# Operands of the Strassen-like groups loaded and split ahead, in a fused attention and MLP block on one core

## The chip, the cores and the metric

The kernel runs on one core of a Trainium2 chip. The metric is the device time of one execution in microseconds (us). The core's engines each work through an instruction queue of their own: TensorE (PE, matmuls), VectorE (DVE), ScalarE (ACT), GpSimd (POOL) and SyncE (SP). SP and POOL issue the DMAs of this kernel, SP nearly all the loads, POOL the adds into memory. All five queues are in order: an instruction that waits holds up what stands behind it.

## The reference

```python
def _A_ref(x, wqkv, wo):            # sliding, dilated local attention
    H, W, dil = 32, 8, 2            # S = 2048 tokens, D = 576, head size 18
    q, k, v = split(x @ wqkv)
    idx = pos[:, None] - arange(W) * dil           # 8 keys, each 2 back
    attn = softmax(q . k[idx] * Dh**-0.5, masked where idx < 0)
    return (attn . v[idx]) @ wo
def _B_ref(x, w1, w2, w3, w4):      # F = 4608
    h  = gelu(layernorm(x) @ w1)
    hs = shift_columns_by_tokens(h) @ w2
    x1 = x + hs
    return x1 + gelu(layernorm(x1) @ w3) @ w4
xn = layernorm(x)
return x + _A_ref(xn, wqkv, wo) + _B_ref(xn, w1, w2, w3, w4)
```

Most of the arithmetic is `gelu(. @ w3) @ w4`. Float32 operands are split into a rounded high part and a low part (their difference), and three products high x high, high x low, low x high stand for one product. Splits are ACT casts followed by DVE subtractions.

## The kernel before, in words

The stages follow each other in one program, whose instructions stand on each engine in the order in which the Python code emits them: order is set by hand.

1. q, k, v products and the two mixer products w1, w2, up to about 313 us. The normalised x1, transposed, is stored as `xn[0..3]`, one DRAM tensor per 512 tokens.
2. 48 *units* u = 0..47. A unit is one pair of 128-wide columns of F (`c`, 12 of them) by one block of 512 tokens (`b`). In unit u PE does the *ups* of u (28 matmuls, line 795), then the four *downs* of unit u-1 (12 matmuls each, line 814). Beside them DVE computes the attention piece by piece (generator `attention`, driven by `bg`); its operands q, k, v come from DRAM over SP, and its output goes to DRAM as `od`. `get_n(b)` loads `xn[b]` for a block's first use, `split_n` splits it. Between u = 5 and 20, sums of blocks of xn are made in DRAM (`td[sb, "T1".."T4"]`).
3. 12 *groups* q = 0..11 cover the other pairs of F columns. One group is a Strassen-like 2 by 2 product: seven products P1..P7 of 7 matmuls each (line 1020), then eight downs D0..D7, which are emitted in the next group (four of unit 47 in q = 0). Groups 0 to 5 take the first half of the tokens (sb = 0), 6 to 11 the second (sb = 1), with the pairs in reversed order. A half has seven operands: `B11` (in P1), `B21` (P2), `T2` (P6), `T1` (P5), `T3` (P7), `T4` (P4), `B22` (P3). `get_op` loads one (two DMAs: 128x2x512, then 96x1x512, which writes the last 32 rows three times), `split_op` splits it. For each pair, `load_pair` loads w3 (raw tile `w3st`, four DMAs), `split_a` makes `w3a`, `combine` and `split_s` make `w3s`; `load_w4` and `split_w4` do the same for w4. All the loads stand in SP's queue, all the casts in ACT's. `ORDER`, `ORDERS` and `plan` say behind which item each of them is emitted.
4. In groups 7 to 10 the attention's output is turned: `load_o` loads a tile of `od` into `big1`, `o_turn` transposes it on DVE into `big0`, `put` stores four of them to `xd`. In group 11 and behind it `read_xo` loads them back, `split_x` and `split_wo` split them and wo.
5. The last eight downs, then the wo products (line 212) and the output.

`negative z` in the code counts from the end: z = u - 48 for the units (z = -3 is unit 45), z = q - 12 for the groups (z = -1 is group 11). A down's output goes to SBUF by a DVE add (line 822), or, for ten of the sixteen token tiles, by an ACT copy to a staging slot (line 818) and an adding POOL DMA into `yd` in DRAM (line 819).

In the kernel before, T2 and T1 of the first half lie in one ring block, T4 and B22 in another, loaded when group 0 begins; for the second half B11 and B21 are loaded in group 4 into `big0` and `big1` (so that B11 and B21 are loaded again in group 6), the others in group 5, where their splits, as those of groups 6, stand beside the downs:

```python
        if q == 0:
            split_s(0)
            x1r = ring_block(("w", 1))
            area["T4"], area["B22"] = x1r[:, 0:5, :], x1r[:, 5:10, :]
            get_op(0, "B22")
            get_op(0, "T4")
            load_pair(1)
```

Of the kernel before, what the change touches and what calls it, by code (L numbers as in the profile page):

```python
# [57 lines left out]
def fused_block(ctx, tc, x, wqkv, wo, w1, w2, w3, w4, out):  # L58
# [476 lines left out]
    def load_w3p(c):  # L535
        st = wspool.tile([128, 4, 3, 128], F32, name="w3st").rearrange("p o s c -> p (o s) c")
        for i in range(2):
            load_w3f(2 * c + i, st[:, 5 * i:5 * i + 5])
# [131 lines left out]
    def attention(ap):  # L670
# [8 lines left out]
        def load(name, sel, g, lead):  # L679
            t = ap.tile([128, TPP + (halo if lead else 0), GC], F32, name=name)  # L680
            r = sel * NG + g
            sp.dma_start(t[:, (halo if lead else 0):, :],
                         qkvd[r, halo:, :].rearrange("(p j) d -> p j d", p=128))
# [28 lines left out]
        qs[0], ks[0] = load("q", 0, 0, False), load("k", 1, 0, True)  # L712
        vs[0] = load("v", 2, 0, True)
# [140 lines left out]
    area = {}  # L854

    def get_op(sb, k):
        n0, n1 = xn[2 * sb], xn[2 * sb + 1]
        src = {"B11": n0[0:HF], "B21": n0[HF:], "B22": n1[HF:]}.get(k)
        if src is None:
            src = td[sb, k]  # L860
        dst = area[k].bitcast(F32)
        sp.dma_start(dst[:, 1:3, :], src[0:256].rearrange("(k p) c -> p k c", p=128))
# [59 lines left out]


# [10 lines left out]
    for u, (c, b) in enumerate(units):  # L934
# [7 lines left out]
        for i in range(C):  # L942
# [4 lines left out]
            if (u, i) == (0, 0):  # L947
                get_n(2, x1n[2])
                load_w3p(1)
            for t in LATE.get((u, i), ()):  # L950
                n_turn(t, ntpool)
            if (u, i) == (0, 1):
                get_n(3, x1n[3])
            if (u, i) in ((1, 0), (2, 1)):
                split_n(u + 1, x1n[u + 1], 0, RT)
            if z == -2:
                split_op(("B11", "B21")[i])
            if z == -1:
# [25 lines left out]
        if z == -3:  # L984
            x2 = xp_tile(2)
            area["B11"], area["B21"] = x2[:, 0:5, :], x2[:, 5:10, :]
            get_op(0, "B11")
            get_op(0, "B21")
            x3 = xp_tile(3)
            area["T3"] = x3[:, 0:5, :]  # L990
            get_op(0, "T3")
        if z == -2:
            x0 = ring_block(("w", 0))
            area["T2"], area["T1"] = x0[:, 0:5, :], x0[:, 5:10, :]
            get_op(0, "T2")
            get_op(0, "T1")
        if 5 <= u < 21 and u % 2:
# [17 lines left out]
    def product(w, xk):  # L1015
        nps[1] += 1
        ps = qpc.tile([128, 512], F32, name=f"cc{nps[1] % 4}")
        for i, (a, v) in enumerate(HALVES):
            k = 128 if a else 96
            pe.matmul(ps, WX[w][:k, v, SLOT[w], :], area[xk][:k, a, :], start=i == 0, stop=i == len(HALVES) - 1)  # L1020
# [5 lines left out]
    x1r = None  # L1026
    otile, xo = {}, {}
    while not state["done"]:
        bg(1e9)
    apc.__exit__(None, None, None)  # L1030


    opc = tc.tile_pool(name="op", bufs=1, reuse_waits="tile")
    opool = opc.__enter__()

    def place(k):
        return opool.tile([128, 5, 512], F32R, name=f"big{k}")

    evc_pool = tc.tile_pool(name="evp", bufs=1, reuse_waits="tile")
    evp = evc_pool.__enter__()  # L1040
# [22 lines left out]
    def o_turn(t):  # L1063
        if t + 3 < NT:
# [7 lines left out]
              NWP: "P1 P2 P6 P5 D0 P7 D1 P4 D2 P3 D3 D4 D5 D6 D7"}  # L1072
    OPS = ("B11", "B21", "T2", "T1", "T3", "T4", "B22")
    for q in range(NQ):
# [50 lines left out]
        run = lambda f, *a: lambda: f(*a)  # L1125
        n = q + 1
        if q == 0:
            plan = {"D0": [run(load_w4, p)], "P5": [run(split_op, "B22")],
                    "P7": [gelu22], "D1": [run(split_op, "T4")],
                    "D2": [run(split_a, n), run(combine, n)], "P3": [run(split_s, n, (0, 1))],  # L1130
                    "P4": [run(split_s, n, (2,)), gelu12, low22],
                    "D3": [run(split_w4, p), low12, run(load_pair, 2)]}
        elif z < -1:
            plan = {"D3": [gelu22], "D4": [low22], "D5": [gelu12], "D6": [low12]}
            late = lambda it, *fs: plan.setdefault(it, []).extend(fs)
            if n != NWP:
                late("P2", run(split_a, n, (0, 1)))
                late("P6", run(split_a, n, (2,)))
                late("D1" if q == 1 else "D0", run(combine, n))
                both = q in (1, NWP)  # L1140
                late("P3", run(split_s, n, (0, 1) if both else (0,)))
                if not both:
                    late("D2", run(split_s, n, (1,)))
                late("D4" if q == 1 else "D3", run(split_s, n, (2,)))
            if q != NWP:
                plan.setdefault("D0", []).insert(0, run(load_w4, p))
                late("D6", run(split_w4, p, 0))
                late("D7", run(split_w4, p, 1))
            if z < -2 and q + 2 != NWP:
                late("D2", run(load_pair, q + 2))  # L1150
        else:
            plan = {"D1": [run(split_w4, p)], "D3": [gelu22], "D4": [gelu12, low22],
                    "D5": [low12]}
            for it, h in (("D2", 0), ("D4", 1)):
                plan.setdefault(it, []).append(lambda h=h: split_x(xo[0], h))
            for it, k in (("P3", 0), ("D3", 1), ("D6", 2)):
                plan.setdefault(it, []).append(run(split_wo, k))
        late = lambda it, *fs: plan.setdefault(it, []).extend(fs)

        def load_ahead(k, op):  # L1160
            x = ahead[op] = place(k)
            mine, area[op] = area[op], x
            get_op(1, op)
            area[op] = mine

        def split_ahead(op):
            mine, area[op] = area[op], ahead[op]
            split_op(op)
            area[op] = mine

        if q == NWP - 2:
            late("P2", run(load_ahead, 0, "B11"))
            late("D1", run(load_ahead, 1, "B21"))
            late("D4", run(split_ahead, "B11"))
            late("D7", run(split_ahead, "B21"))
        if q == NWP - 1:
            for it, k in zip(("P6", "P5", "P7", "P4", "P3"), OPS[2:]):
                plan.setdefault(it, []).insert(0, run(get_op, 1, k))
            for it, k in zip(("D2", "D4", "D6"), OPS[2:5]):
                late(it, run(split_op, k))  # L1180
        if q == NWP:
            late("P2", lambda: area.update(own), run(get_op, 1, "B11"), run(split_op, "T4"))
            late("P6", run(get_op, 1, "B21"))
            late("D0", run(split_op, "B22"))
            late("D5", run(split_op, "B11"))
            late("D7", run(split_op, "B21"))
# [3 lines left out]
        if -4 <= z <= -2:  # L1190
            plan.setdefault("P1", []).insert(0, run(put, ("o", z + 4)))
        if z == -2:
            late("D7", run(put, ("o", 3)))
# [5 lines left out]
        if z == -1:  # L1199
            late("P2", lambda: read_xo(0, xp_tile(2)))  # L1200
            late("P5", lambda: read_xo(1, ring_block(("o", 1))))
            late("P7", lambda: read_xo(2, xp_tile(3)))
            late("P3", lambda: read_xo(3, ring_block(("o", 3))))
# [112 lines left out]
```

## Time and profile before

| what | us |
|---|---|
| median of 3 runs (lowest, highest) | 1348.0 (1347.28, 1349.06) |
| the profiled execution's own time | 1341.79 |
| its span | 1340.0 |
| PE busy in the span | 1290.5 (96%) |
| DVE, ACT, POOL busy | 954.2, 550.9, 211.4 |
| one group with nothing in its way (q = 2, 978.15 to 1002.17) | 24.02 |

PE is busy nearly all the time, so time is lost where PE stands idle, and where it runs at a lower granted clock afterwards (column PEclk, 1.00 is full). A row of the timeline reads: start, duration, engine, line, operation, tiles, count, and in brackets the idle time before it with what ended it. A row of the windows reads: window, length, busy time of each engine with its count of instructions, granted clock, busy share of the 16 DMA engines (a row's share can pass 1 a little, since a packet counts in the slice in which it starts), GB/s.

### The profile page before, as it was taken

The page shows a single profiled execution, that of the slowest core. Times are in us where ns is not written, and L with a number is a line of the kernel's source. Part 1 is how long each engine was busy: PE and PEld are TensorE (multiplying, and loading weights), DVE is VectorE, ACT ScalarE, POOL GpSimd, SP SyncE. Part 2 cuts the span into 40 slices and gives each one's busy share as a digit, 9 for nine tenths or more (in the row PEclk, how much of TensorE's full clock was granted, in tenths as well). Part 3 has the DMA queues.
Part 4 walks back from the last instruction along what each step waited for, and adds up shares of the span by engine and source line. Part 5 has one row for each costly group of instructions (what it writes and reads, how often), then busy time and mean ns, then how long its engine had stood idle before and what let it go on. Part 6 is the DMA issues. An engine that isn't in the chain of part 4 may idle for free.

```text
span 1340.0 us, 19496 instructions
## 1 busy us (share of the span) xinstructions
PE 1290.5 (96%) x7594; PEld 1182.2 (88%) x7594; DVE 954.2 (71%) x1359; ACT 550.9 (41%) x882; POOL 211.4 (16%) x310
## 2 busy tenths in 40 slices
PE   9999999999899999999999999999899969989698
PEld 8999998898799989989999999888799958978698
DVE  6445525877378999899999999776766747657432
ACT  4332136446334434334343434336454645533520
POOL 2011100021112212122122221111021111211100
PEclk9999999999899999999999999999999989999799
DMA  7637874158786796978786874667566765878952
GB/s 214 154 100 158 185 161 145 48 152 220 211 204 105 151 270 102 228 134 185 146 188 129 172 156 77 130 140 167 126 107 157 149 161 123 189 168 193 292 140 80
DMA packets 195119, 211.66 MB, mean 158 GB/s; under 512 B 75906, under 2 KB 132162, under 8 KB 194898
## 3 DMA queue, kind: packets, MB, share of 16 engines
q1 hardware_dynamic: 165234, 149.65, 38.2%
q0 software_dynamic: 29792, 60.76, 30.2%
q8 instruction: 59, 0.97, 0.3%
q14 instruction: 34, 0.28, 0.1%
HBM read 114.43 MB, written 107.28 MB: 165 GB/s over the span
## 4 chain that ended last, share of the span: by engine, by line
PE 57%; issue 8%; DVE 2%; DMA 2%; SPq 2%; POOL 1%; ACT 1%; POOLq 0%; DVEq 0%; ACTq 0%
PE ps L814 27%; PE p L795 21%; PE cc L1020 5%; PE ps L212 4%; DMA w3st<-in_B_w_dram 1%; POOL yd L819 1%; SPq L890 1%; SPq L888 1%; DMA yd<-Y 1%; DVE prod L703 0%; PE p L1283 0%; DVE xt L587 0%; DVE Y L822 0%; ACT ev L818 0%; DVE Y L1024 0%
## 5 line engine op out<-in xcount | busy, mean ns | idle before, releaser
L814 PE MATMUL ps<-w,c 128*128 128x288 f32 x3456 | 483.9, 298 | 26.7 <-ACT Y L818 12.1
L814 PEld LDWEIGHTS ps<-w,c 128*128 128x128 f32 x3456 | 475.4, 191 | 38.4 <-ACT Y L818 12.9
L819 POOL DMA_DIRECT2D yd<-Y x128 | 112.7, 885 | 486.7 <-ACT Y L818 468.1
L818 ACT COPY Y<-ps 128x576 f32<-128x576 f32 x128 | 81.6, 639 | 170.4 <-PE ps L814 83.4
L789 DVE TENSOR_TENSOR c<-Y,c 128x512 fp32r<-128x512 f32 x144 | 98.6, 686 | 72.3 <-ACT Y L779 61.1
L778 ACT ACTIVATE c<-p 128x512 fp32r<-128x512 f32 x96 | 57.4, 597 | 194.6 <-PE p L795 194.6
L212 PE MATMUL ps<-WQ,xt 128*128 128x432 f32 x672 | 134.8, 360 | 0.0
L212 PEld LDWEIGHTS ps<-WQ,xt 128*128 128x128 f32 x672 | 125.7, 188 | 5.5
L822 DVE TENSOR_TENSOR Y<-ps,Y 128x576 f32<-128x576 f32 x108 | 81.1, 752 | 13.5 <-PE ps L814 13.3
L723 DVE TENSOR_TENSOR prod<-q,k 128x1152 f32<-128x1152 f32 x64 | 86.6, 1353 | 0.9
L726 DVE TENSOR_REDUCE L<-prod 128x64 f32<-128x1152 f32 x64 | 86.4, 1350 | 0.9
L819 POOL DMA_DIRECT2D yd<-ev x52 | 45.3, 876 | 249.2 <-ACT ev L818 247.6
L795 PE MATMUL p<-xt,w3a 128*128 128x512 f32 x336 | 78.9, 392 | 1.4 <-ACT Y L779 1.4
L795 PE MATMUL p<-x1n,w3a 128*128 128x512 f32 x336 | 79.3, 393 | 0.0
L795 PE MATMUL p<-x1n,w3s 128*128 128x512 f32 x336 | 78.7, 391 | 0.0
L795 PE MATMUL p<-xt,w3s 128*128 128x512 f32 x336 | 78.5, 391 | 0.0
L707 DVE TENSOR_TENSOR o<-o,prod 128x1152 f32<-128x1152 f32 x56 | 75.8, 1354 | 0.9
L703 DVE TENSOR_TENSOR prod<-v,L 128x1152 f32<-128x1152 f32 x56 | 75.7, 1352 | 0.5
L795 PEld LDWEIGHTS p<-xt,w3a 128*128 128x128 f32 x336 | 62.3, 188 | 14.8 <-ACT Y L779 2.2
L795 PEld LDWEIGHTS p<-x1n,w3a 128*128 128x128 f32 x336 | 63.1, 190 | 12.8
L795 PEld LDWEIGHTS p<-x1n,w3s 128*128 128x128 f32 x336 | 62.4, 188 | 12.8 <-DVE w3s L198 0.3
L1024 DVE TENSOR_TENSOR Y<-cc,Y 128x512 f32<-128x512 f32 x84 | 56.2, 687 | 24.5 <-PE cc L1020 23.9
(184 smaller groups left out, 1759.3 us busy)
## 6 DMA issues: line engine op xcount, KB each, us to landing
yd<-Y POOLq DMA_DIRECT2D x128, 288.0 KB, 5.3
yd<-ev POOLq DMA_DIRECT2D x52, 288.0 KB, 6.7
Y<-in_B_w_dram SPq DMA_DIRECT2D x23, 576.0 KB
w3st<-in_B_w_dram SPq DMA_DIRECT2D x44, 256.0 KB
qkvd<-stg SPq DMA_DIRECT2D x24, 432.0 KB
xd<-st SPq DMA_DIRECT2D x16, 320.0 KB
xd<-big SPq DMA_DIRECT2D x16, 320.0 KB
xin<-in_A_x_dram SPq DMA_DIRECT2D x16, 288.0 KB
```

What stands on the lines that cost most here:

```text
L212: pe.matmul(ps[:, h, :n], xs(a), ws(b, h), start=i == 0, stop=i == len(PAIRS) - 1)
L703: dve.tensor_tensor(dst, vv, Lf[:, :, w:w + 1].to_broadcast([128, TPP * GH, HD]), op=ALU.mult)
L707: dve.tensor_tensor(o, o, dst, op=ALU.add)
L723: dve.tensor_tensor(prod.rearrange("p (j h) d -> p j (h d)", h=GH), q, k[:, r0:r0 + TPP, :], op=ALU.mult)
L726: dve.tensor_reduce(Lf[:, :, w], prod, axis=AX.X, op=ALU.add)
L789: dve.tensor_tensor(h[:, 1, :], g, h[:, 0, :].bitcast(F32), op=ALU.subtract)
L795: pe.matmul(ps, W3[f][:, w, :], x1n[b][:, a, :], start=n == 0, stop=n == len(PAIRS) - 1)
L814: pe.matmul(ps[:, k, :HF], h[:, col], w[:, p, k * HF:(k + 1) * HF], start=n == 0, stop=n == len(seq) - 1)
L818: act.copy(e.rearrange("p (h c) -> p h c", h=2), ps[:, :, :HF])
L819: pool.dma_start(yd[t], e, accum_op=ALU.add)
L822: dve.tensor_tensor(yv, ps[:, :, :HF], yv, op=ALU.add)
L1020: pe.matmul(ps, WX[w][:k, v, SLOT[w], :], area[xk][:k, a, :], start=i == 0, stop=i == len(HALVES) - 1)
```

## The change

1. The attention's first loads of q, k and v move from SP's queue to POOL's, and are issued behind the second down of unit 3's turn; the second half of `load_w3p(1)` is issued one step later.
2. Room: at the end of unit 45 the attention's pool is closed (its rows on DVE end there in both kernels), and T4 and B22 of the first half are loaded into `big0` and `big1` in that room. The loads of pair 1's w3 stand behind them at the same place; w4 of group 0 follows behind unit 46, pair 2's w3 behind unit 47. Splits of T3, T4, T2, T1 and of w3, w4 are emitted in units 46 and 47, that of B22 in group 0.
3. The second half's operands: T4 and B22 are loaded and split in groups 2 and 3, into the ring block that is now free; B11, B21, T2, T1 and T3 are loaded once, in group 5 behind the product that reads the slot last, and split at D0, D2, D4, D7 of group 5 and D1 of group 6. Group 6 begins with two downs. Pair 7's w3 is loaded in group 4.
4. In groups 7 to 10 `o_turn` stands behind D1, D2, D5, D6 (before: D2, D4, D6, D7), and `put` behind D7 of the same group.
5. In group 11 `split_w4` moves one down later, and splits of wo and of the turned tiles move from the group to the last eight downs.

```diff
-    def load_w3p(c):
+    def load_w3p(c, part=(0, 1)):
...
-        qs[0], ks[0] = load("q", 0, 0, False), load("k", 1, 0, True)
-        vs[0] = load("v", 2, 0, True)
+        yield None
+        qs[0], ks[0] = load("q", 0, 0, False, pool), load("k", 1, 0, True, pool)
+        vs[0] = load("v", 2, 0, True, pool)
...
-                load_w3p(1)
+                load_w3p(1, (0,))
...
             if (u, i) == (0, 1):
+                load_w3p(1, (1,))
                 get_n(3, x1n[3])
...
             if z == -2:
-                split_op(("B11", "B21")[i])
+                split_op(0, ("B11", "B21")[i])
             if z == -1:
-                split_op(("T3", "T2")[i])
+                split_op(0, ("T2", "T1")[i])
         for j, (t, parts) in enumerate(prev):
             bg(r, j == 1)
             down(t, parts, psb)
+            if (u, j) == (3, 1):
+                next(state["gen"])
...
-            if z == -1 and j == 2:
-                split_op("T1")
+            for f in {(-3, 1): (lambda: split_a(0),), (-3, 3): (lambda: combine(0),),
+                      (-2, 1): (lambda: split_op(0, "T3"),), (-2, 3): (lambda: split_op(0, "T4"),),
+                      (-1, 0): (lambda: split_s(0, (0, 1)),), (-1, 1): (lambda: split_s(0, (2,)),),
+                      (-1, 2): (lambda: split_w4(NPL),),
+                      (-1, 3): (lambda: split_a(1),)}.get((z, j), ()):
+                f()
...
         if z == -3:
...
+            while not state["done"]:
+                bg(1e9)
+            apc.__exit__(None, None, None)
...
+            area[0].update(T4=place(0), B22=place(1))
+            for k in ("B11", "B21", "T3", "T4", "B22"):
+                get_op(0, k)
+            load_pair(1)
         if z == -2:
+            load_w4(NPL)
             x0 = ring_block(("w", 0))
...
             get_op(0, "T2")
             get_op(0, "T1")
+        if z == -1:
+            x1 = ring_block(("w", 1))
+            area[1].update(T4=x1[:, 0:5, :], B22=x1[:, 5:10, :])
+            load_pair(2)
...
-              NWP: "P1 P2 P6 P5 D0 P7 D1 P4 D2 P3 D3 D4 D5 D6 D7"}
+              NWP: "D0 D1 P1 P2 D2 P6 D3 P5 P7 D4 P4 P3 D5 D6 D7"}
...
+        elif q == NWP - 1:
+            at("P1", load_w4, p)
+            for it, k in zip(("P1", "P2", "P6", "P5", "P7"), ("B11", "B21", "T2", "T1", "T3")):
+                at(it, get_op, 1, k)
+            at("D0", split_op, 1, "B11")
+            at("D2", split_op, 1, "B21")
...
+            at("D4", split_op, 1, "T2")
...
+            at("D5", split_w4, p, 0)
...
+            at("D6", split_w4, p, 1)
+            at("D7", split_op, 1, "T1")
...
+        if q in (2, 3):
+            k = ("T4", "B22")[q - 2]
+            at("P2", get_op, 1, k)
+            at("D5", split_op, 1, k)
         if -5 <= z <= -2:
-            for i, it in enumerate(("D2", "D4", "D6", "D7")):
-                late(it, run(o_turn, 4 * (z + 5) + i))
...
+            for i, it in enumerate(("D1", "D2", "D5", "D6")):
+                at(it, o_turn, 4 * (z + 5) + i)
+            at("D7", put, ("o", z + 5))
...
+        if j in (0, 2):
+            split_x(xo[0], j // 2)
         if j in (1, 4):
-            split_x(xo[1], j // 3)
-        if j in (0, 3):
             split_wo(3 + j // 3)
+        if j == 6:
+            split_x(xo[1], 0)
```

The first place is SP's queue from unit 45 to group 0. In it `x1n3` is T3's slot, `xt_8403` (before) and `xt_8433` (after) that of T2 and T1, `xt_8540` and `big0`, `big1` those of T4 and B22, `w3st_8545` and `w3st_8310` hold pair 1's w3, `Y_71` is w4's staging. Before:

```order
L862 DMA x1n3_8294<-td0T3_102 128x2x512
L863 DMA x1n3_8294<-td0T3_102 96x1x512
L862 DMA xt_8403<-td0T2_101 128x2x512
L863 DMA xt_8403<-td0T2_101 96x1x512
L862 DMA xt_8403<-td0T1_100 128x2x512
L863 DMA xt_8403<-td0T1_100 96x1x512
L862 DMA xt_8540<-xn1_97 128x2x512
L863 DMA xt_8540<-xn1_97 96x1x512
L862 DMA xt_8540<-td0T4_103 128x2x512
L863 DMA xt_8540<-td0T4_103 96x1x512
L888 DMA w3st_8545<-in_B_w3_dram 128x2x256
L890 DMA w3st_8545<-in_B_w3_dram 96x1x256
```

After, behind T3's two rows, on the same engine:

```order
L865 DMA big0_8298<-td0T4_103 128x2x512
L866 DMA big0_8298<-td0T4_103 96x1x512
L865 DMA big1_8299<-xn1_97 128x2x512
L866 DMA big1_8299<-xn1_97 96x1x512
L892 DMA w3st_8310<-in_B_w3_dram 128x2x256
L894 DMA w3st_8310<-in_B_w3_dram 96x1x256
L892 DMA w3st_8310<-in_B_w3_dram 128x2x256
L894 DMA w3st_8310<-in_B_w3_dram 96x1x256
L555 DMA Y_71<-in_B_w4_dram 128x2x576
L865 DMA xt_8433<-td0T2_101 128x2x512
L866 DMA xt_8433<-td0T2_101 96x1x512
L865 DMA xt_8433<-td0T1_100 128x2x512
```

T4, B22, pair 1's w3 and group 0's w4 now stand ahead of T2 and T1; before, they stood behind.

The second place is ACT's queue in unit 47. `c21`, `c11` are the gelus of its two ups, `ps` the outputs of unit 46's downs, `w3s` the split of pair 0's w3. Before:

```order
L778 ACTIVATE c11_8447<-p1_8432 128x512
L779 ACTIVATE Y_71<-p1_8432 128x512
L870 ACTIVATE xt_8403<-xt_8403 128x1024
L871 ACTIVATE Y_71<-xt_8403 32x512
L872 ACTIVATE xt_8403<-xt_8403 64x512
L818 COPY Y_71<-ps_8470 128x576
L818 COPY Y_71<-ps_8485 128x576
```

After:

```order
L873 ACTIVATE xt_8433<-xt_8433 128x1024
L874 ACTIVATE Y_71<-xt_8433 32x512
L875 ACTIVATE xt_8433<-xt_8433 64x512
L781 ACTIVATE c11_8477<-p1_8462 128x512
L782 ACTIVATE Y_71<-p1_8462 128x512
L873 ACTIVATE xt_8433<-xt_8433 128x1024
L874 ACTIVATE Y_71<-xt_8433 32x512
L875 ACTIVATE xt_8433<-xt_8433 64x512
L907 CAST w3s_8500<-w3st_8174 128x1024
L909 CAST w3s_8500<-w3st_8174 96x512
L821 COPY Y_71<-ps_8503 128x576
L821 COPY Y_71<-ps_8520 128x576
```

Both splits of the slot `xt` (T2, then T1) now stand ahead of the copies of unit 46's downs; before, only T2's did, and T1's stood between the copies.

The third place is ACT's queue where the first half passes into the second (end of group 5, begin of group 6): `ev` are copies of downs, `c11`, `c22`, `c12`, `c21` the group's gelus, `w3a` the split of pair 7. Before, in group 6:

```order
L784 ACTIVATE c21_9886<-Y_71 128x512
L785 ACTIVATE Y_71<-Y_71 128x512
L1207 COPY Y_71<-cc3_9889 128x512
L903 CAST w3a_9908<-w3st_9778 128x768
L905 CAST w3a_9908<-w3st_9778 96x384
L870 ACTIVATE xt_8540<-xt_8540 128x1024
L871 ACTIVATE Y_71<-xt_8540 32x512
L872 ACTIVATE xt_8540<-xt_8540 64x512
```

After, from the end of group 5 on:

```order
L562 CAST w4_9668<-Y_71 128x2x576
L821 COPY ev4_9865<-ps1_9852 128x576
L821 COPY ev0_9883<-ps0_9870 128x576
L873 ACTIVATE xt_8433<-xt_8433 128x1024
L874 ACTIVATE Y_71<-xt_8433 32x512
L875 ACTIVATE xt_8433<-xt_8433 64x512
L787 ACTIVATE c21_9891<-Y_71 128x512
L788 ACTIVATE Y_71<-Y_71 128x512
L821 COPY ev1_9921<-ps0_9908 128x576
L873 ACTIVATE x1n3_8297<-x1n3_8297 128x1024
L874 ACTIVATE Y_71<-x1n3_8297 32x512
L875 ACTIVATE x1n3_8297<-x1n3_8297 64x512
```

In the kernel before, the casts of pair 7's w3 stand ahead of T4's split (`xt_8540`) in group 6; after, no split of T4 or B22 is left there, T1's and T3's stand around copies of downs.

More of the change, by code (lines that the diff above doesn't have):

```diff
@@ L533, in load_w3f @@
         dup_tail(raw[:, 4, :], w3, f * 128, 128)
-    def load_w3p(c):
-        st = wspool.tile([128, 4, 3, 128], F32, name="w3st").rearrange("p o s c -> p (o s) c")
-        for i in range(2):
-            load_w3f(2 * c + i, st[:, 5 * i:5 * i + 5])
+    def load_w3p(c, part=(0, 1)):
+        if 0 in part:
+            t = wspool.tile([128, 4, 3, 128], F32, name="w3st")
+            raws["pair"] = t.rearrange("p o s c -> p (o s) c")
+        for i in part:
+            load_w3f(2 * c + i, raws["pair"][:, 5 * i:5 * i + 5])
     def split_w3(f):
@@ L677, in attention, with load @@
         qs, ks, vs, Ls, den = {}, {}, {}, {}, {}
-        def load(name, sel, g, lead):
+        def load(name, sel, g, lead, sp=sp):
             t = ap.tile([128, TPP + (halo if lead else 0), GC], F32, name=name)
@@ L884, in load_pair @@
         c0 = 2 * (NPL + pair(q)) * 128
-        st = WS["st", q] = (evp if q % 2 else wspool).tile([128, 3, 4, 128], F32, name="w3st")
+        odd = (q - (q > NWP)) % 2
+        st = WS["st", q] = (evp if odd else wspool).tile([128, 3, 4, 128], F32, name="w3st")
         for k in range(2):
@@ L921, in split_s, with place @@
         split_ws(WS[q], WS["st", q], steps)
+    def place(k):
+        return opool.tile([128, 5, 512], F32R, name=f"big{k}")
     units = [(c, b) for c in range(NPL) for b in (range(NB) if c < NPL - 1 else (2, 3, 0, 1))]
@@ L1019, in product @@
             k = 128 if a else 96
-            pe.matmul(ps, WX[w][:k, v, SLOT[w], :], area[xk][:k, a, :], start=i == 0, stop=i == len(HALVES) - 1)
+            pe.matmul(ps, WX[w][:k, v, SLOT[w], :], area[sb][xk][:k, a, :], start=i == 0, stop=i == len(HALVES) - 1)
         return ps
@@ L1024, in z_add @@
         dve.tensor_tensor(by_token(dst), in_order(ps), by_token(z), op=ALU.add)
-    x1r = None
     otile, xo = {}, {}
[L1028 to L1040, printed above, removed]
     EV[0] = None
     Wo = None
-    ahead = {}
     worw = {}
@@ L1124, in fused_block, with at @@
         low12 = lambda: low_part(hid[q, "c12"], Z2)
-        run = lambda f, *a: lambda: f(*a)
         n = q + 1
+        plan = {}
+        def at(it, f, *args):
+            plan.setdefault(it, []).append(lambda: f(*args))
         if q == 0:
[L1128 to L1132, printed above, removed]
-        elif z < -1:
[L1134 to L1150, printed above, removed]
-        else:
[L1152 to L1186, printed above, removed]
@@ L1187, in fused_block @@
-        if -5 <= z <= -2:
-            for i, it in enumerate(("D2", "D4", "D6", "D7")):
-                late(it, run(o_turn, 4 * (z + 5) + i))
[L1190 to L1193, printed above, removed]
+            at("P2", split_op, 0, "B22")
+            at("D0", combine, n)
+            at("P7", gelu22)
+            at("D2", low22)
+            at("P3", split_s, n, (0, 1))
+            at("P4", gelu12)
@@ new lines, in fused_block @@
+            at("P4", split_s, n, (2,))
+            at("D3", low12)
+        elif q == NWP - 1:
[4 more added lines that the diff above has]
+            at("D2", split_op, 1, "B21")
+            at("D3", gelu22)
+            at("D4", low22)
+            at("D4", split_op, 1, "T2")
+            at("D5", gelu12)
+            at("D5", split_w4, p, 0)
+            at("D6", low12)
+            at("D6", split_w4, p, 1)
+            at("D7", split_op, 1, "T1")
+        elif q == NWP:
+            at("D1", split_op, 1, "T3")
+            at("P2", split_a, n, (0, 1))
+            at("P6", split_a, n, (2,))
+            at("D3", combine, n)
+            at("D4", gelu22)
+            at("D4", load_pair, q + 2)
+            at("P4", low22)
+            at("P3", split_s, n, (0, 1))
+            at("D5", gelu12)
+            at("D5", split_s, n, (2,))
+            at("D6", low12)
+        elif z < -1:
+            at("P2", split_a, n, (0, 1))
+            at("P6", split_a, n, (2,))
+            at("D0", load_w4, p)
+            at("D1" if q == 1 else "D0", combine, n)
+            if q == 1:
+                at("P3", split_s, n, (0, 1))
+            else:
+                at("P3", split_s, n, (0,))
+                at("D2", split_s, n, (1,))
+            at("D3", gelu22)
+            at("D4" if q == 1 else "D3", split_s, n, (2,))
+            at("D4", low22)
+            at("D5", gelu12)
+            at("D6", low12)
+            at("D6", split_w4, p, 0)
+            at("D7", split_w4, p, 1)
+            if z < -2:
+                at("D2", load_pair, q + 2 + (q == NWP - 2))
+        else:
+            at("D2", split_w4, p)
+            at("D3", gelu22)
+            at("D4", low22)
+            at("D4", gelu12)
+            at("D5", low12)
+            for k, it in enumerate(("D5", "D6", "D7")):
+                at(it, split_wo, k)
@@ L1199, in fused_block @@
         if z == -1:
[L1200 to L1203, printed above, removed]
+            at("P2", lambda: read_xo(0, xp_tile(2)))
+            at("P5", lambda: read_xo(1, ring_block(("o", 1))))
+            at("P7", lambda: read_xo(2, xp_tile(3)))
+            at("P3", lambda: read_xo(3, ring_block(("o", 3))))
         for it in ORDERS.get(q, ORDER).split():
@@ L1263, in fused_block @@
         yv = Y[:, t, :].rearrange("p (h c) -> p h c", h=2)
+        if t == 0:
+            split_x(xo[1], 1)
         if t in (1, 2):
```

39 lines of the change are left out of this document (13 added, 26 removed).

## The prediction

> **What bounds the kernel now.** I read the page first, for the share of PE.
>
> ```profile
> span 1340.0 us, 19496 instructions
> PE 1290.5 (96%) x7594; PEld 1182.2 (88%) x7594; DVE 954.2 (71%) x1359; ACT 550.9 (41%) x882; POOL 211.4 (16%) x310
> PEclk9999999999899999999999999999999989999799
> ```
>
> PE is the bound: it can only win back its idle time and the low clock behind it (the 8 and 7 of the last line). Of the sum below the base is the profiled execution, 1341.79 us with a span of 1340.0; it lies 6.2 us under the median of the runs, 1348.0, so I carry the gain over to the median. A run of this kernel tells a difference from no change at about 0.2%, 2.7 us.
>
> Next I cut the part with the groups into windows, one per group, from P1 to the next P1.
>
> ```profile
> core 0: us, PE busy (x) PEld busy (x) DVE busy (x) ACT busy (x) POOL busy (x), PEclk, DMA share, GB/s
> 928.86:947.23 18.37, 17.96 (x100) 15.51 (x98) 13.98 (x17) 12.73 (x20) 2.25 (x3) 1.00 0.76 178
> 947.23:978.15 30.92, 26.29 (x148) 23.50 (x147) 23.18 (x42) 15.29 (x25) 3.85 (x5) 0.94 0.41 84
> 978.15:1002.17 24.02, 24.02 (x146) 21.95 (x146) 16.16 (x27) 11.97 (x20) 4.36 (x6) 1.00 0.62 116
> 1074.47:1115.35 40.88, 29.20 (x147) 24.77 (x146) 21.20 (x34) 19.31 (x29) 4.35 (x5) 0.83 0.64 157
> 1115.35:1141.79 26.44, 24.84 (x147) 21.70 (x146) 21.01 (x36) 15.20 (x25) 4.58 (x6) 1.00 0.54 110
> 1165.81:1195.21 29.40, 25.99 (x148) 23.07 (x146) 19.35 (x37) 12.22 (x20) 4.49 (x6) 0.94 0.80 182
> 1195.21:1224.55 29.34, 26.07 (x147) 23.43 (x146) 18.95 (x35) 12.19 (x20) 4.34 (x6) 0.94 0.76 171
> 1224.55:1277.16 52.61, 41.86 (x243) 38.31 (x242) 25.07 (x33) 23.02 (x36) 8.72 (x11) 0.87 0.92 245
> ```
>
> Group 2 (978.15) shows what a group costs when nothing is late: 24.02. Against it group 1 loses 6.9, group 6 16.9, group 7 2.4, groups 9 and 10 5.4 and 5.3. Group 0 has only four downs; with the 6.50 of four downs (row 922.51 below) taken off 24.02, its 18.37 loses 0.8. The last window is group 11 with the last eight downs, 24.02 + 2 x 6.4 = 36.8, so 52.61 loses about 15.8. Then the waits of PE inside, from its timeline.
>
> ```profile
> 350.39 3.25 PE L814 MATMUL ps<-w,c 128*128 128x288 f32 x12 [4.76 <-ACT Y L818]
> 353.43 7.29 PE L795 MATMUL p<-x1n,w3a 128*128 128x512 f32 x28
> 916.13 6.55 PE L795 MATMUL p<-xt,w3s 128*128 128x512 f32 x28
> 922.51 6.50 PE L814 MATMUL ps<-w,c 128*128 128x288 f32 x48
> 954.39 0.53 PE L814 MATMUL ps<-w,c 128*128 128x288 f32 x2 [3.77 <-ACT w L560]
> 1096.02 3.76 PE L1020 MATMUL cc<-xt,w3a 128*128 128x512 f32 x7 [8.77 <-ACT xt L870]
> 1177.87 3.33 PE L1020 MATMUL cc<-xt,w3a 128*128 128x512 f32 x7 [2.23 <-DVE Y L1024]
> 1244.86 2.43 PE L814 MATMUL ps<-w,c 128*128 128x288 f32 x12 [2.47 <-DVE Y L822]
> 1251.80 11.90 PE L814 MATMUL ps<-w,c 128*128 128x288 f32 x72 [4.51 <-ACT Y L818]
> 1266.56 3.25 PE L814 MATMUL ps<-w,c 128*128 128x288 f32 x12 [2.86 <-ACT Y L818]
> ```
>
> A wait costs more than its bracket: seven matmuls behind the 2.23 at 1177.87 took 3.33, though 28 of the same shape take 6.55 (1.64 for seven). The Trainium skill ("TensorE: Matmul & The Clock Gate", Part 1) says that the clock halves after an idle window of some 3.4 us; here it is low after 2.23 already, so I go by the rows and count windows, not brackets. At the start, unit 3, the loss is 4.76 + (3.25 - 1.6) + (7.29 - 6.55) = 7.1. All losses that the change touches: 7.1 + 7.7 + 19.3 + 10.7 + 15.8 = 60.6.
>
> **The start: +4 of 7.1.** SP's, ACT's and DVE's timelines:
>
> ```profile
> 340.54 0.69 SPq L682 DMA_DIRECT2D q<-qkvd  x1
> 347.59 0.63 ACT L596 ACTIVATE Y<-x1n 64x512 fp32r<-64x512 f32 x1 [5.60 <-DMA x1n<-xn]
> 363.90 1.35 DVE L723 TENSOR_TENSOR prod<-q,k 128x1152 f32<-128x1152 f32 x1
> ```
>
> The q, k, v loads stand right behind x1n[3]'s and share its bandwidth; ACT waits 5.60 for x1n[3], and the down's copy (line 818) behind it holds PE. Moved to POOL behind unit 3's second down, they start only when that split is done, so the wait shrinks to about 1, that is 6 of the 7.1 back. The price: q and k land later, about when unit 4 starts, and DVE's first attention row, which stood at 363.90, waits with unit 4's other DVE rows behind it. Nothing in this trace has q and k on POOL's queue. Bounds: 0 (they land in the gaps of DVE) to 5 (DVE loses the whole wait of x1n[3] again); I take 2, since DVE has gaps in unit 4. POOL's own yd adds behind those loads lose a few us, covered by the three staging slots. Bounds of the term 1 and 6.5.
>
> **From the units into group 0: -5, where 7.7 were lost.** The change wants T4, B22, w3, w4 ready before group 0, so that group 1's waits (3.77 on w4's cast in the rows above) go. But they now stand ahead of T2 and T1 in SP's queue. What an operand's load costs there:
>
> ```profile
> 897.25 1.07 SPq L862 DMA_DIRECT2D x1n<-td0T  x1
> 909.98 0.37 SPq L862 DMA_DIRECT2D xt<-td0T  x1
> 922.71 0.36 SPq L862 DMA_DIRECT2D xt<-xn  x1
> 925.61 7.40 SPq L890 DMA_DIRECT2D w3st<-in_B_w_dram  x1
> 933.05 4.18 SPq L888 DMA_DIRECT2D w3st<-in_B_w_dram  x1
> DMA  5499996799885396799941149979993222222129
> GB/s 91 122 324 362 416 347 221 208 365 359 208 183 145 82 135 118 161 211 239 253 118 69 69 116 145 132 117 203 196 216 91 76 59 47 53 47 54 40 53 164
> ```
>
> The first five are issues of SP; the last two are the DMA's busy tenths and GB/s in 40 slices from 911 to 924. Read the run of 2s: for the last stretch only a fifth of the 16 engines work, at 40 to 59 GB/s. These are the second pieces, 96x1x512, 192 KB an operand: at some 53 GB/s 3.6 us each, one behind the other. The Trainium skill ("DMA: Bandwidth & Descriptors", "Why a DMA increments its semaphore by 16 and not by 1") says that a hardware-generated DMA runs on the largest number of engines that divides its slowest dimension, here 3, and on the lowest-numbered ones each time; 3 of 16 is .19, and the 2s agree. By it, all second pieces queue on the same three, which speaks against putting more of them ahead of T2; by all 16 engines (the 300 to 400 GB/s of the early slices) T4, B22 and w3 would take 3 x 1.9 = 6 us for 704 KB each, and T2 would come in time. T2 and T1, issued at 909.98, are through at about 924, 14 us for two operands beside the yd adds; B22 and T4, issued at 922.71, hold SP's later issues (7.40, 4.18) until 937, again 14. ACT meets T1 just in time:
>
> ```profile
> 921.60 0.63 ACT L871 ACTIVATE Y<-x1n 32x512 fp32r<-32x512 f32 x1
> 923.74 1.05 ACT L870 ACTIVATE xt<-xt 128x1024 fp32r<-128x1024 f32 x1
> 926.01 0.62 ACT L818 COPY Y<-ps 128x576 f32<-128x576 f32 x1
> ```
>
> After the change T4, B22 and a w3 pair (as many bytes on those engines as one operand) go first. Behind T3 that is 3 x 3.6 = 11 us at the bare rate and 3 x 7 = 21 at the rate beside the adds; I take 14, nearer the bare rate, since adds stop when PE does. T1 is then ready near 938, not 924. ACT blocks on T2 and T1, and behind them stand unit 47's second gelu and the copies of unit 46's downs (926.01 above); PE has two output buffers of slack, so it stands still for about 12 and loses 1 more to the clock. Against that the 7.7 go. 7.7 - 13 is -5; bounds +6.5 (T2 in time, 1.2 of the old waits left) and -13 (21 us late).
>
> **Groups 5 to 7: +13.5 of 19.3.** Now ACT waits here:
>
> ```profile
> 1092.65 0.83 ACT L903 CAST w3a<-w3st 128x768 fp32r<-128x768 f32 x1 [10.11 <-DMA w3st<-in_B_w_dram]
> ```
>
> Pair 7's w3 stands behind seven operand loads; T4's split, which releases the 8.77 of PE, stands behind that cast. After, the w3 comes in group 4, T4 and B22 in groups 2 and 3 (DMA share .62 in group 2 leaves room), and five operands remain. Between their issue (from 1052 on) and their use stand w4 and five times 3.6 to 7 us, 18 to 35 us: T1 is due at 1077, T3 near 1081. I expect ACT to be late by about 4 and w4's low half by 2, so 5.8 remain. Bounds: 1 left (18.3 back) and 10 left (9 back). The added group-2 and group-3 splits (four ACT and two DVE pieces each, 2.3 us of ACT in a group where it is busy 11.97 of 24.02) cost nothing.
>
> **Groups 8 to 10: +8.5 of 10.7.** DVE's turns wait for od:
>
> ```profile
> 1159.57 12.79 SPq L1060 DMA_DIRECT2D big<-od  x4
> ```
>
> The four loads stood behind `put`, and each is issued only when its slot is free. Moved up by one or two downs, with `put` behind D7 of its own group, they are spread over the group; DMA share .80 and .76 shows that the engines are well filled already, so I leave 2.2. Bounds 0 and 6 left.
>
> **The end: +11 of 15.8.**
>
> ```profile
> 1249.01 0.61 ACT L178 CAST x1n<-x1n 64x512 fp32r<-64x512 f32 x1 [6.96 <-DMA x1n<-xd]
> ```
>
> This wait goes since split_x moves behind the last downs' first; with it 4.51 of PE, and 2.47 with w4's split. The 2.86 at 1266.56 stays: there ACT waits for staging slots, which the change does not touch, and the DMA share .92 stays. The slow clock costs 41.86 - 36.8 = 5.1, of which some 4 go. 2.47 + 4.51 + 4 = 11. Bounds 7 and 14.
>
> **Sum.** 4 - 5 + 13.5 + 8.5 + 11 = 32. 1341.8 - 32 = 1309.8 on the profiled execution, 1348 - 32 = 1316 on the median. That is the forecast.
>
> **Rivals.**
>
> *T2 and T1 are in time.* If the three engines drain between the adds as fast as the early stretch of the slices (300 to 400 GB/s), the stall does not come and the term is its upper bound, +6.5 in place of -5: 32 + 11.5 = 43.5, 1304.5. For it: SP is idle from 898 to 910, so T4 and B22 start in a gap. Against it: the run of 2s. Chance .22.
>
> *The five operands of the second half are late as well.* In group 5 they queue on the same three engines behind w4, and T2's, T1's and T3's splits stand ahead of copies and gelus, so each us late is a us of PE. At 7 us an operand 10 more would be lost: 32 - 10 = 22, 1326. For it: the 14 us for two operands. Against: no unit's adds run as densely in the products of group 5. Chance .20.
>
> *Slower: the attention lags.* DVE's load beside the units:
>
> ```profile
> 600.00:620.00 20.00, 20.00 (x125) 18.41 (x124) 18.79 (x20) 7.16 (x13) 2.87 (x4) 1.00 0.73 158
> ```
>
> It is busy 18.79 of 20, and its start slips by some 8 us. If every unit's DVE rows then hold PE a little, it decides from 32 / 41 units = 0.8 us per unit on; at 1.0 a unit 41 are lost: 1357. Against: PE is busy 20.00 of 20 in that window, and the attention's rows are dealt out per down, whatever their start. Chance .04.
>
> *It doesn't do what it says:* the operands come ahead, but every wait moves to the next one and the sum is nought, 1348. Chance .03.
>
> **How the numbers follow.** The forecast has .51, the rivals .22, .20, .04 and .03. 1316 is the likeliest case's time; its own range, from the bounds of the terms with two of them at an end, is 1308 to 1324. The range takes in the first two rivals and a spread of 7 about each: 1298 to 1333. Faster: .51 + .22 + .20 = .93; same .03; slower .04.
>
> **What would show it.** In the profile after: T1's split on ACT in unit 47 with a wait for a DMA of 10 or more, and PE idle behind it, in the forecast and the second rival; none in the first. Unit 3's wait of ACT for x1n[3] near 1, with DVE's first prod waiting for q or k. No wait on w3st in group 6, and group 6 near 28 in place of 40.88. Groups 9 and 10 near 25. From group 11's P1 to the first wo product near 41. I am wrong if the loads ahead of T2 do not delay it, or if the turns still wait for od.

## The result, and the profile after

The changed kernel takes 1328.45 us in the median of four runs (1327.41 to 1335.34), the kernel before 1347.86 (four runs, 1347.28 to 1349.06): a ratio of 0.9866, 95% interval 0.9831 to 0.9900. Forecast were 1316, with a range of 1298 to 1333. In the profiled executions the gain is smaller, 1340.0 to 1325.7 in the span, 14.3, because that of before lay 6 us under its median and that of after (1327.43 by its own time) 1 us under. All stages below are differences of these two traces.

First the page, then PE's waits after the change, from its timeline.

```profile
span 1325.7 us, 19467 instructions
PE 1279.8 (97%) x7594; PEld 1175.7 (89%) x7594; DVE 951.2 (72%) x1355; ACT 546.2 (41%) x876; POOL 214.3 (16%) x315
PEclk9999999999999999999999999999799999989999
```

```profile
349.17 1.85 PE L817 MATMUL ps<-w,c 128*128 128x288 f32 x12 [3.13 <-ACT Y L821]
363.59 6.55 PE L798 MATMUL p<-xt,w3s 128*128 128x512 f32 x28
401.33 1.85 PE L817 MATMUL ps<-w,c 128*128 128x288 f32 x12 [0.99 <-DVE Y L825]
887.36 1.85 PE L817 MATMUL ps<-w,c 128*128 128x288 f32 x12 [1.26 <-DVE Y L825]
942.52 3.25 PE L817 MATMUL ps<-w,c 128*128 128x288 f32 x12 [16.71 <-DVE Y L825]
1085.40 1.85 PE L817 MATMUL ps<-w,c 128*128 128x288 f32 x12 [2.08 <-ACT ev L821]
1185.22 8.95 PE L817 MATMUL ps<-w,c 128*128 128x288 f32 x48 [6.44 <-DVE Y L825]
1214.23 8.15 PE L817 MATMUL ps<-w,c 128*128 128x288 f32 x48 [2.40 <-DVE Y L825]
1254.17 1.85 PE L817 MATMUL ps<-w,c 128*128 128x288 f32 x12 [1.33 <-ACT Y L821]
```

The 7 in PEclk is the slice of the 16.71. That one wait, new in this kernel, is larger than any of before. The 8.77 in group 6 and the 4.51 in group 11 have gone; the 4.76 in unit 3 has become 3.13, with another of 1.48 at 333.05. The windows of the groups (the same columns as in the prediction; group 6 begins with two downs now, so the row of group 5 is longer and that of group 6 shorter by two downs):

```profile
945.57:964.38 18.81, 18.81 (x98) 16.43 (x98) 14.53 (x25) 10.26 (x16) 1.95 (x3) 0.93 0.61 132
964.38:988.40 24.02, 24.02 (x148) 21.93 (x147) 16.80 (x29) 11.44 (x19) 3.70 (x5) 1.00 0.48 99
1060.38:1092.05 31.67, 28.24 (x171) 25.22 (x170) 20.10 (x25) 20.05 (x31) 5.92 (x7) 1.00 0.89 198
1092.05:1112.90 20.85, 20.85 (x124) 18.76 (x122) 15.91 (x28) 11.52 (x19) 2.84 (x4) 1.00 0.62 146
1112.90:1136.92 24.02, 24.02 (x148) 21.93 (x146) 17.51 (x33) 11.63 (x19) 4.36 (x6) 1.00 0.60 130
1136.92:1160.94 24.02, 24.02 (x148) 21.93 (x146) 19.26 (x36) 11.98 (x20) 4.34 (x6) 1.00 0.90 194
1160.94:1194.00 33.06, 26.62 (x147) 24.30 (x146) 19.25 (x36) 11.97 (x20) 4.35 (x6) 0.90 0.75 168
1194.00:1222.23 28.23, 25.83 (x148) 23.51 (x147) 19.26 (x36) 11.97 (x20) 4.36 (x6) 0.94 0.74 158
1222.23:1262.66 40.43, 37.78 (x244) 34.74 (x242) 21.98 (x31) 20.96 (x34) 8.70 (x11) 1.00 1.04 280
```

Groups 1, 6, 7 run without a wait, where they lost 6.9, 16.9 and 2.4. Group 9 became slower, 29.40 to 33.06. By stages, from one mark in both timelines to the next (the timeline of before has P1 of group 2 at 977.99, 0.16 ahead of the mark in the prediction's windows):

| stage (marks before / after) | before | after | gain | forecast |
|---|---|---|---|---|
| to the downs in unit 44's turn (888.99 / 887.36) | 888.99 | 887.36 | +1.6 | +4 |
| to P1 of group 2 (977.99 / 988.40) | 89.00 | 101.04 | -12.0 | -5 |
| to P1 of group 8 (1141.79 / 1136.92) | 163.80 | 148.52 | +15.3 | +13.5 |
| to P1 of group 11 (1224.55 / 1222.23) | 82.76 | 85.31 | -2.6 | +8.5 |
| to the wo products (1277.16 / 1262.66) | 52.61 | 40.43 | +12.2 | +11 |
| to the end | 62.84 | 63.04 | -0.2 | 0 |
| sum | | | +14.3 | +32 |

How the 16.71 comes about is seen on ACT and DVE, on SP, and on the DMA's busy tenths and GB/s in 40 slices from 922 to 938:

```profile
933.46 1.06 ACT L873 ACTIVATE xt<-xt 128x1024 fp32r<-128x1024 f32 x1 [10.97 <-DMA xt<-td0T]
936.48 0.62 ACT L874 ACTIVATE Y<-xt 32x512 fp32r<-32x512 f32 x1 [1.96 <-DMA xt<-td0T]
940.34 0.62 ACT L874 ACTIVATE Y<-xt 32x512 fp32r<-32x512 f32 x1 [0.67 <-DMA xt<-td0T]
934.55 1.23 DVE L589 SCALAR_TENSOR_TENSOR xt<-xt 128x1024 fp32r<-128x1024 f32 x1 [11.34 <-ACT xt L873]
941.70 0.76 DVE L825 TENSOR_TENSOR Y<-ps,Y 128x576 f32<-128x576 f32 x1
```
```profile
901.22 4.30 SPq L866 DMA_DIRECT2D big<-td0T  x1
914.51 6.62 SPq L892 DMA_DIRECT2D w3st<-in_B_w_dram  x1
923.81 1.17 SPq L865 DMA_DIRECT2D xt<-td0T  x1
```
```profile
DMA  8851128979996999458995211121112211122121
GB/s 164 292 166 60 77 100 134 279 279 385 345 260 227 312 328 328 161 161 250 372 293 197 85 77 72 72 77 72 72 72 77 77 72 72 72 77 77 67 77 72
```

SP is held up while it issues T4 and pair 1's w3 (4.30, 6.62), so T2 is issued only at 923.81, 14 later than the 909.98 of before. From 931 on what is left comes in at 67 to 77 GB/s with a tenth or two of the engines busy, and ACT waits for T2 (10.97 for its first piece, 1.96 for its second) and for T1's last piece until 940.34. DVE, which subtracts behind each cast, waits for ACT (11.34). The add that empties a down's output, and so releases PE, stands on DVE behind both splits (941.70), and the ACT copies of the other downs come behind it.

### The profile page after: what moved, and what is told of

It is laid out like the page before. It is cut to its first block, busy times and chain, and to the rows that moved or that the text cites. A ratio compares the mean times of both kernels' runs of the same rounds, so it can differ in the third digit from the quotient of the medians.

```text
span 1325.7 us, 19467 instructions
## 1 busy us (share of the span) xinstructions
PE 1279.8 (97%) x7594; PEld 1175.7 (89%) x7594; DVE 951.2 (72%) x1355; ACT 546.2 (41%) x876; POOL 214.3 (16%) x315
## 4 chain that ended last, share of the span: by engine, by line
PE 51%; issue 8%; DMA 5%; DVE 5%; POOL 2%; SPq 1%; ACT 0%; POOLq 0%; DVEq 0%; ACTq 0%
PE ps L817 23%; PE p L798 17%; PE cc L1045 7%; PE ps L212 4%; POOL yd L822 1%; DMA big<-xn 1%; DVE prod L705 1%; DMA xt<-td1T 1%; DMA xt<-td0T 1%; DVE o L709 1%; DMA v<-qkvd 1%; SPq L865 1%; DVE prod L726 1%; DVE L L729 1%; DMA k<-qkvd 1%
## 5 line engine op out<-in xcount | busy, mean ns | idle before, releaser
L798 PEld LDWEIGHTS p<-xt,w3s 128*128 128x128 f32 x336 | 62.4, 188 | 12.6
```

Source lines behind the costliest of these rows:

```text
L798: pe.matmul(ps, W3[f][:, w, :], x1n[b][:, a, :], start=n == 0, stop=n == len(PAIRS) - 1)
```

## The experiments

All are edits of the changed kernel, unless said otherwise, timed against the kernel before; spans are of one profiled execution each, against 1325.7 and 1340.0. They were taken in three groups, in which the kernel before took 1345.29, 1347.51 and 1347.67, and the four executions of the changed kernel alone differ by 8 us. So ratios compare better than spans, and a difference of 2 or 3 us between two spans says little.

**Second pieces on 16 engines.** Theory: the 96-row pieces go through three engines only.

```diff
-        sp.dma_start(dst[0:96, 0, :], dram_ap(src, 256 * 512, [[0, 3], [512, 32], [1, 512]]))
+        for r in range(3):
+            sp.dma_start(dst[32 * r:32 * r + 32, 0, :], src[256:288])
```

The same in `load_pair`.

> The changed kernel, but the second piece of each operand and of each w3 pair (96 rows, 3 engines) is loaded as three DMAs of 32 rows. Theory A, three engines are the bottleneck: T2 and T1 land before ACT needs them (921 to 925), the 16.71 us stall of PE at the last unit falls to 3 or less, groups 5 and 6 lose 3 less; span 1325.7 to about 1308. Rival B, the place in the queue and the bytes count, not the engines: T2 lands 3 us earlier at most, the stall stays at 12 or more, span 1320 or above.

1314.07 us, ratio 0.9774 (0.9760 to 0.9789), span 1311.6. PE's stall fell from 16.71 to 5.42; the row and its cause on ACT:

```profile
934.01 3.25 PE L817 MATMUL ps<-w,c 128*128 128x288 f32 x12 [5.42 <-DVE Y L825]
926.17 1.06 ACT L874 ACTIVATE xt<-xt 128x1024 fp32r<-128x1024 f32 x1 [4.38 <-DMA xt<-td0T]
916.78 0.44 SPq L865 DMA_DIRECT2D xt<-td0T  x1
```

Same bytes, same order, three DMAs in place of each second piece for SP to issue, and two thirds of the stall gone, though not down to the 3 of theory A: the shape of these pieces made that part of it. SP isn't held any more and issues T2 at 916.78, 7 earlier. Group 5 gains too: 29.16 (1051.80 to 1080.96) for 31.67. The rest of the stall is in the main a wait for T2's first piece; that the bytes ahead of it cause that is shown further down, where they are moved.

**w3 and w4 behind T2 and T1**, engines as in the changed kernel (`load_pair(1)` and `load_w4(NPL)` moved behind `get_op(0, "T1")`).

> The changed kernel, but pair 1's w3 and group 0's w4 are loaded behind T2 and T1 instead of ahead. Theory A: of the 10 us that T2 is waited for at first, the w3 and w4 pieces on the three engines make 6 to 7; the stall falls from 16.71 to about 10, and some 2 come back as waits for w3 or w4 in groups 0 and 1; span about 1321. Rival: T4 and B22 alone fill the queue until 933, the stall stays above 14. Another rival: the queue order is no matter at all, stall 16 to 17.

1324.54 us, 0.9852 (0.9837 to 0.9867), span 1323.3. The stall is 11.67, so those two made 5 of it, a little under the estimate. The stage up to group 2 gained as much (985.22 less 889.58 is 95.64, for 101.04), and the waits expected in groups 0 and 1 did not come. The span gained only 2.4: this execution came to unit 44's downs 2.2 later and lost 3.0 more in group 5 (34.67), and gained 2.2 in groups 8 to 10.

**The turns where they were.** Group 9 lost time in the changed kernel because DVE's first turn waits for `put`, the store of the previous four tiles, which still reads the buffer that the turn writes:

```profile
1161.37 16.77 SPq L166 DMA_DIRECT2D xd<-big  x4
1183.01 0.71 DVE L158 STREAM_TRANSPOSE big<-big 128x512 f32<-128x512 f32 x1 [7.78 <-DMA xd<-big]
```

In the kernel before, with the turns at D2, D4, D6 and D7, the wait was for the load of `od`, whose last stretch runs with two tenths of the engines busy (its turn, then the DMA's busy tenths and GB/s in 40 slices from 1160 to 1176):

```profile
1175.73 0.71 DVE L158 STREAM_TRANSPOSE big<-big 128x512 f32<-128x512 f32 x1 [8.09 <-DMA big<-od]
DMA  9999999899733989999979999989952222222222
GB/s 350 248 228 224 252 359 284 183 227 247 167 107 97 134 112 166 180 225 210 173 150 207 202 179 127 132 156 196 213 110 69 69 69 69 58 63 69 81 104 104
```

```diff
-            for i, it in enumerate(("D1", "D2", "D5", "D6")):
+            for i, it in enumerate(("D2", "D4", "D6", "D7")):
```

> The changed kernel, but the turns of the attention's output stand behind D2, D4, D6, D7 again, put behind D7 of the same group as changed. Theory C, the first turn now comes while put still reads the turned buffer: DVE's waits at line 158 (7.8 and 3.7 us) fall below 2 each, group 9 from 33.06 to about 25, group 10 from 28.23 to about 25; span about 1315. Rival D, od is late as before: DVE waits for od instead, 4 to 8 us a group, and groups 9 and 10 stay at 28 or more; span 1323 to 1326.

1332.58 us, 0.9905 (0.9891 to 0.9920), span 1331.2. The waits for `put`, 7.78 and 3.74, shrink to 1.21 and 3.26, and the one for `od` is back, as the rival had it:

```profile
1176.02 0.71 DVE L158 STREAM_TRANSPOSE big<-big 128x512 f32<-128x512 f32 x1 [8.20 <-DMA big<-od]
1204.82 0.71 DVE L158 STREAM_TRANSPOSE big<-big 128x512 f32<-128x512 f32 x1 [7.60 <-DMA big<-od]
```

Groups 8 to 10 together take 85.76 (1141.97 to 1227.73), for 85.31 in the changed kernel; most of the rest of the 5.5 in span was lost ahead of them, where the two kernels are the same. So two waits lie on top of each other, and the place of the turns chooses between them. Both are waits for a DMA.

**od on 16 engines.** Turns as changed, each load of `od` (outer dimension 4) as four DMAs of 32 rows.

```diff
-        sp.dma_start(otile[t],
-                     dram_ap(od, (512 * b + 32 * i) * D, [[128 * D, 4], [D, 32], [1, D]]))
+        for r in range(4):
+            sp.dma_start(otile[t][32 * r:32 * r + 32],
+                         dram_ap(od, (512 * b + 32 * i + 128 * r) * D, [[D, 32], [1, D]]))
```

> The changed kernel, but each load of od (four parts of 32 rows, 4 engines) is issued as four DMAs of 32 rows. Theory E, put is slow because its pieces queue behind od loads on four engines: SP's put at 1161.37 (16.77 us to issue) falls to about 9, DVE's waits at line 158 to 2 or less, groups 9 and 10 at about 25; span about 1315. Rival F, put is slow by its own 512-byte rows: put still takes 9 to 14, the wait stays at 4 or more; span 1321 or above.

1317.81 us, 0.9804 (0.9779 to 0.9829), span 1315.5. SP's `put`, which took 16.77 to issue, takes 5, and groups 8 to 10 run clean (SP's row, then windows):

```profile
1164.62 4.96 SPq L166 DMA_DIRECT2D xd<-big  x4
```
```profile
1140.17:1164.19 24.02, 24.02 (x147) 21.94 (x146) 19.26 (x36) 11.98 (x20) 4.36 (x6) 1.00 0.99 221
1164.19:1188.21 24.02, 24.02 (x147) 21.93 (x146) 19.27 (x36) 11.99 (x20) 4.37 (x6) 1.00 0.97 221
1188.21:1212.23 24.02, 24.02 (x147) 21.93 (x146) 19.27 (x36) 11.99 (x20) 4.36 (x6) 1.00 0.79 161
```

Theory E held beyond its number (9 was expected): `put` was slow because it stood behind the `od` loads in their old shape, not by its own rows.

**The attention's first loads on SP again**, as in the kernel before (the `pool` argument and the late `next` taken out; the second half of `load_w3p(1)` stays where the change put it).

> The changed kernel with the attention's first loads of q, k and v on SP's queue again, as in the kernel before. Theory G, x1n[3] waits for its own store and load, not for q, k, v: ACT still waits about 4 to 6 for x1n[3], PE about 4 to 5 there, the ups of unit 4 start near 367 as in the other runs, DVE's 9.94 us wait for k and PE's 1 us near 401 go; span within 2 of the changed kernel's. Rival H, the loads share its bandwidth: PE's wait grows by 3 or more over 3.13 to 5.40, unit 4 starts at 370 or later, span 3 to 4 longer.

1331.53 us, 0.9885 (0.9852 to 0.9918), span 1325.6. Unit 3's wait, on ACT and PE:

```profile
347.28 0.63 ACT L598 ACTIVATE Y<-x1n 64x512 fp32r<-64x512 f32 x1 [4.71 <-DMA x1n<-xn]
350.08 3.25 PE L816 MATMUL ps<-w,c 128*128 128x288 f32 x12 [3.88 <-ACT Y L820]
```

PE's wait is no longer than with the loads on POOL: 3.13 in the changed kernel, 4.05 to 5.40 in the eight runs of kernels built on it. With the loads on SP there are three traces: 3.88 here, 4.76 in the kernel before and 6.18 in a run further down, so the two sets overlap. In the changed kernel DVE waited for k until 370.61 (9.94); here its first row stands at 362.98. No slowing of x1n[3] by the loads behind it in its queue shows; one of about 1 us is not excluded.

**The kernel before, nothing moved, all those pieces on 16 engines.**

> The kernel before, with nothing moved, but the second pieces of operands and w3 pairs and the loads of od issued as DMAs of 32 rows (16 engines). If the three and four engines were what made the operands late there too, groups 9 and 10 fall from 29.4 to about 24.5, group 6 from 40.88 to about 30, group 1 from 30.92 to about 27; span 1340 to about 1315. If the order of the loads was what cost, as the change takes it, groups 1 and 6 keep most of their loss and only groups 9 and 10 gain: span about 1328.

1320.27 us, 0.9802 (0.9784 to 0.9820), span 1318.4. Groups 8 to 10 take 24.02 each, group 6 27.4 (P1 at 1075.57, the next at 1102.97) in place of 40.88. Group 1 keeps its loss (30.21), with the old wait for w4, and group 7 keeps its 26.4:

```profile
955.47 0.53 PE L814 MATMUL ps<-w,c 128*128 128x288 f32 x2 [3.20 <-ACT w L560]
```

So the shape of the DMAs alone is worth more (27.2 by the medians, 21.6 of span) than the whole reordering without it (19.4 and 14.3); but groups 1 and 7 and the end (1201.45 to 1255.05, 53.6) needed the reordering.

**Both, on the changed kernel.**

> The changed kernel with both: second pieces of operands and w3, and od, on 16 engines. If the two add up, 1325.7 less 14 less 10 is a span of about 1302: stall at the last unit near 5.4, groups 8 to 10 at 24.02. If they compete (shorter pieces of one kind only move the queue to the other), 1308 or more.

1302.59 us, 0.9666 (0.9645 to 0.9686), span 1302.3. They add up: the stall is 4.66, groups 8 to 10 take 24.02 each. On top of the new shape the reordering takes the ratio from 0.9802 to 0.9666, as much as it took without it (1 to 0.9866).

**And B22, w3, w4 behind T2 and T1.**

> As the run before, and B22, pair 1's w3 and group 0's w4 are loaded behind T2 and T1. The rest of the stall (5.42) is bytes ahead of T2: 704 KB twice and 576 KB at some 300 GB/s are 6 us, so the stall falls to 1 or less and the span to about 1297, if B22 and w4 still come in time for group 0; if they are late, PE waits 2 to 4 in group 0 and the span stays near 1301.

1296.41 us, 0.9617 (0.9598 to 0.9636), span 1294.5. The stall is gone, so it was the bytes ahead that T2 still waited for. PE's last wait ahead of group 0 is this one, and none shows in group 0:

```profile
929.17 1.85 PE L817 MATMUL ps<-w,c 128*128 128x288 f32 x12 [0.18 <-DVE Y L825]
```

**On that kernel, w3's half behind x1n[3]** (`get_n(3)` ahead of `load_w3p(1, (1,))`).

> As the fastest run so far (all pieces on 16 engines; B22, w3 and w4 behind T2 and T1; span 1294.5), but the second half of w3's pair 1 is loaded behind x1n[3] instead of ahead. Theory: x1n[3] waits for the bytes ahead of it in SP's queue and for the adds beside it, so 320 KB less ahead take 1 to 2 off ACT's wait of 5.13 and off PE's 4.29; span about 1293. Rival: x1n[3] waits for its own store into DRAM and for the adds alone; the wait stays at 4.5 to 5.5.

1296.35 us, 0.9620 (0.9602 to 0.9637), span 1294.0. ACT's wait for x1n[3] is 5.16, PE's 4.33: the rival's numbers. The 320 KB that stood ahead of it in its queue are not what holds it either. What is left, its own store or POOL's adds beside it, was not told apart.

**On that kernel, the turns where they were before.**

> As the fastest run so far (span 1294.5), but the turns stand behind D2, D4, D6, D7 again. If the four engines alone held the turns, the places do not matter: groups 8 to 10 stay at 24.02 each, span 1294 to 1296. If the places matter on their own, groups 9 and 10 lose 2 or more each, span 1298 or above.

1295.58 us, 0.9615 (0.9598 to 0.9632), span 1293.8, no different from 1296.41. Groups 8 to 10 take 24.02 each. Once `od` runs on all engines, the places of the turns are worth nothing that shows.

## Why the prediction was right or wrong

The sign and the range held; the likeliest time was 12 us too low, and the gain of 19.4 by the medians was 0.6 of the 32 forecast. That the range held is partly luck: on the two profiled executions, from which the sum was worked out, the gain was 14.3, which taken off 1348 is 1333.7, just beyond the range. The time lies near the second rival's 1326, but what that rival described did not happen. Two terms made most of the miss, that of group 0 (7 too high) and that of groups 8 to 10 (11 too high).

- **Units into group 0: the mechanism right, the size short.** T2 and T1 late behind T4, B22, w3 and w4, ACT blocked, PE idle: as written, with DVE as the link between. Groups 0 and 1 gave back 6.3 (49.13 to 42.83) of the 7.7 forecast. The term mis-sized is "I take 14": T1's last piece was cast at 940.34, against the 924 by which the DMA of before was through with T2 and T1, less the 1.6 already gained. So it was some 18 late, within the bounds of 11 to 21, and PE stood 16.71 instead of 12. The reason given for the low end, that adds stop when PE does, came too late to help: until 923 SP could not even issue T2. One reading of a line was wrong: the cast at 923.74 is T2's. T1's stands between the copies, as the order in the second place of the change has it:

```profile
928.00 1.06 ACT L870 ACTIVATE xt<-xt 128x1024 fp32r<-128x1024 f32 x1
```

- **Groups 8 to 10: the step failed.** It said that loads spread over the group would leave 2.2; instead the stage lost 2.6, outside the bounds of 4.7 to 10.7. The forecast looked at the wait for `od`, which went, and not at the next one: it had `put` behind D7 and the first turn at D1, but never asked whether `put` is through by then. The shape of the `od` loads was the cause of both, as the runs with 32-row loads and either place of the turns show. The thought that the first boundary was weighed by, which DMAs stand behind slow ones, was not applied here.
- **The start: the step failed, cheaply.** ACT's wait for x1n[3] was to shrink from 5.60 to about 1, and was still 3.96; sharing the bandwidth with the loads behind it made at most about 1 of it, by the run with these loads on SP. What makes the rest stays open. The 1.6 is no proof of a gain: the nine kernels with this start came to unit 44's downs between 887.36 and 891.63, the three with q, k and v on SP at 888.45, 888.99 and 890.65. DVE did wait 9.94 for k, and PE's wait in the next units is 0.99, less than the 2 allowed; so the third rival, that the attention lags, did not come.
- **Groups 5 to 7: the size right**, 15.3 for 13.5, and 4.5 of loss left for 5.8. But T1 and T3, which were to be late, were not waited for: ACT waited 6.68 for B11, 1.36 for B21 and 1.58 for T2, and PE behind them and behind w4's cast 2.08, 0.92 and 0.33. The second rival asked for 10 more and did not come.
- **The end: right**, 12.2 for 11. The waits of 2.47 and 4.51 went; of the wait for staging slots 2.86 became 0.96 and 1.33.

Two small slips changed nothing: the start's upper bound is 6 by its own figures, not 6.5, and an added split has three ACT pieces, not four.

## What to carry to other kernels

Before moving loads ahead in a queue, ask what then stands behind them and when that is needed, and on how many engines each runs: here a DMA whose outer dimension is 3 or 4 held up the whole queue while most engines idled, and slices with a tenth or two of DMA busy, at 40 to 104 GB/s, were its mark. Writing the same bytes as DMAs of 32 rows was worth 27.2 us by the medians in the kernel before, with nothing moved, and the reordering brought as much on top of it as without it. Only when B22, w3 and w4 went behind T2 and T1 as well did the stall that the reordering had made go, for 6 us more. When a stall is taken away, follow the buffer to the next instruction that must wait for it, here the store that still reads what the next turn writes.

## What the runs showed of the hardware

The Trainium skill ("DMA: Bandwidth & Descriptors", "Why a DMA increments its semaphore by 16 and not by 1") ties the number of engines to the outer dimension; the runs agree: with 3 the last pieces ran at 67 to 77 GB/s with a tenth or two of the engines busy, and dividing them in DMAs of 32 rows took the ratio from 0.9866 to 0.9774. The trace does not name the engines, so that all such pieces share the same ones is not shown. The runs add how far it spreads: SP itself is held when it issues into such a queue (4.30 and 6.62 us for single issues, where T2's took 0.44 in the run with 32-row pieces; 16.77 for the four of `put`, where they took 4.96 behind 32-row loads of `od`), so DMAs of other shapes behind it come late too. Also, PE ran 12 matmuls in 1.85 behind idle times of 3.13 in the changed kernel, but in 3.25 behind 4.05 and 3.88 in two of the other runs, and seven in 3.33 behind 2.23 in the kernel before: the idle time alone did not say whether the clock falls.
